# A new hand-laid order of the steps in a pooled-attention-and-two-MLPs kernel, with fourteen small steps on another engine

## The chip, the cores and the metric

One core of a Trainium2 chip. The metric is the device time of one execution of the program in microseconds (us), a median over runs. PE is the matrix engine (TensorE), DVE the vector engine, ACT the scalar engine, POOL the GpSimd engine, SP the engine that issues the DMA transfers here.

## What is computed

Pooled attention, then a gated MLP behind an RMS norm, then a second MLP, all in fp32 accuracy:

```python
k_p = k.reshape(B, H, 72, 8, D).mean(axis=3)      # B=4, H=8, S=576, D=64
v_p = v.reshape(B, H, 72, 8, D).mean(axis=3)
scores = q @ k_p.T / sqrt(D)
attn = exp(scores - scores.max(-1)); attn /= attn.sum(-1) + 1e-9
x = (attn @ v_p).transpose(0, 2, 1, 3).reshape(2304, 512)
xn = x / sqrt((x * x).mean(-1) + 1e-6) * rms_g
y = (silu(xn @ w_gate) * (xn @ w_val)) @ w_out    # 512 -> 1536 -> 512
out = silu(y @ w_in) ; out = out @ w_out2         # 512 -> 2048 -> 512
```

The reference computes silu as g / (1 + exp(-g)). The weights arrive as float64.

## The kernel before

**Tiling.** The 2304 tokens are eight chunks of 288 for the attention, with scores in pieces of 96 queries by 72 pooled keys. The gated MLP runs over chunks 0 to 4, and for the rest in two wide passes of 432 columns (called 8 and 9). The second MLP runs over three thirds of 768 tokens (a, b, c) with seven products in place of eight for a two-by-two block product. A product in fp32 accuracy is three matmuls on split numbers, high times high, high times low, low times high (`mm3`, L257 to L259; L773 in the second MLP). So each operand is split on another engine first: a rounded copy (`copy`, L237 on ACT or L239 elsewhere) and the difference from it (`combine`, L244).

**Weights.** A block of weights comes by one DMA of 512 KB of float64 words (`w_load`, L155) and is turned to fp32 by bit operations: `w_low` (L171), `w_scale` (L237), `w_sign` (on ACT L186, on DVE L178), `w_join` (L190), then the split, high (L237 or L239) and low (L244).

**Order.** Nothing orders the steps but a text. Four strings, `start`, `pair`, `last` and `second`, hold 3981 tokens; `play` goes through them and each token advances one generator by one step, which issues its instructions on their engines' queues. Each engine executes its queue in order and waits at an instruction until its inputs and its tile are there. A token is a chunk (none means 0), a letter for the kind of step, an index, and at will an engine (`:v` DVE, `:g` POOL, `:a` ACT) for its copy or difference:

```python
for o in order.split():
    o, _, e = o.partition(":")
    ...
    engine[0] = e or None
    if key not in begun:
        begun[key] = begin(*key)
    next(begun[key], None)
```

So `4H7:g` is the next step of chunk 4's eighth value tile, with its difference on POOL. The letters that matter here: K, V, Q load keys, values and queries (L276, L283 to L293, L307); k and a sum the pooled keys and values (L342 or L338, and L358 or L325 with L329) and lay them into `kbd` and `vbd`; m and s are score products (PE, L405) and the softmax's maximum (DVE, L416) and six exponentials with one small scaling (ACT, L423, L428); w divides by the sum, p transposes the weights on PE (L456), x multiplies them with the values and leaves square and raw output (L498, L237 `xraw`), r and n normalise; Z stores them. B is a weight block. G, H, D are the gate, value and output products of the first MLP; after H stands the product with the gate (L642, or L814 in a wide pass) and the split of `hT` or `hw`, which D multiplies. Y stores an MLP output (L677). Over the hand-over to the second MLP, L loads and converts a block of its output weights, S and E form their sums and splits and store them (L758), X reads the first MLP's output back (L852) and sums it (L865). A, B, C load, sum and split a block of input weights, U is its product, J and T split the hidden tile, W is the last product.

**Queues.** SP issues nearly all DMAs, in the order of the text; a load whose tile is still read, or a store whose data isn't there, holds back all behind it. Score and transposition tiles of the chunks after the first share two PSUM banks (tag `att`, two buffers): a transposition can have to wait until the exponentials have read an older score tile.

Of the kernel before, what the change touches and what calls it, by code (L numbers as in the profile page):

```python
# [22 lines left out]
def tile_pooled_attention_then_two_mlps(  # L23
# [239 lines left out]
    p1 = ctx.enter_context(tc.tile_pool(name="p1", bufs=1))  # L263
# [441 lines left out]
    p2, pw, p2x = [], [], []  # L705
# [139 lines left out]
    x2 = {}  # L845
# [148 lines left out]
    def down2(c, m):  # L994
# [112 lines left out]
    )  # L1107
# [248 lines left out]
```

## Time and profile before

| | us |
|---|---|
| median of three runs | 937.98 (937.88 to 938.92) |
| the profiled execution | 935.67 |
| its span | 933.9 |
| PE busy | 902.3 (97%), 6122 matmuls |
| DVE busy | 628.0 (67%) |
| ACT busy | 544.0 (58%) |
| POOL busy | 367.2 (39%) |

A busy share is a mean over stages that have different limits. PE's idle time (31.6 us of the span) is at the beginning, at a few waits in the middle and at the hand-over to the second MLP. A view by stretches of time gives each engine's busy time per stretch, the share of full speed that the clock of TensorE was granted (1.00 is 2.4 GHz, 0.50 is 1.2 GHz) and the share of DMA time. The view of waits says for which instruction of which engine PE waited. A timeline gives single instructions: start, length, engine, line, operation, result and operand, and in brackets the idle time before it and what ended it.

### The profile page before, as it was taken

How to read it: one execution, taken by the hardware profiler on the slowest of the kernel's cores; microseconds unless marked ns; L12 is line 12 of the kernel's file. 1: busy time of each engine (PE TensorE's matmuls, PEld its weight loads, DVE VectorE, ACT ScalarE, POOL GpSimd, SP SyncE). 2: the span in 40 equal slices, each digit the busy share in tenths (PEclk: the TensorE clock that was granted, in tenths of full speed). 3: DMA queues.
4: the chain of work that ended last, by engine and by line, in shares of the span. 5: the costliest groups of instructions: out<-in, count | busy, mean ns of one | idle time of the engine just before them, and what ended most of it. 6: DMA issues, size and time to landing. Idle time of an engine off the chain costs nothing.

```text
span 933.9 us, 17344 instructions
## 1 busy us (share of the span) xinstructions
PE 902.3 (97%) x6122; PEld 876.5 (94%) x6122; DVE 628.0 (67%) x1255; ACT 544.0 (58%) x1456; POOL 367.2 (39%) x485
## 2 busy tenths in 40 slices
PE   5999899999998999999999999999999999999998
PEld 4688899999998989999999898999999999999998
DVE  6889988756544643543466779667986669866675
ACT  5687887365252723335534546776766767667653
POOL 6544242444213541200026555892028930289200
PEclk9789999999999999999999999999999999999999
DMA  8745641442114402144466885355872568724386
GB/s 255 224 154 155 215 132 52 128 136 91 50 50 112 121 29 81 45 139 146 155 216 221 292 279 196 95 203 181 258 239 69 204 182 258 238 68 159 116 263 209
DMA packets 85259, 149.79 MB, mean 160 GB/s; under 512 B 8627, under 2 KB 53812, under 8 KB 85172
## 3 DMA queue, kind: packets, MB, share of 16 engines
q1 hardware_dynamic: 85172, 148.68, 49.5%
q8 instruction: 48, 0.79, 0.4%
q14 instruction: 39, 0.32, 0.1%
HBM read 116.21 MB, written 32.44 MB: 159 GB/s over the span
## 4 chain that ended last, share of the span: by engine, by line
PE 76%; DVE 10%; DMA 5%; POOL 3%; issue 2%; ACT 2%; SPq 1%; ACTq 0%; DVEq 0%; POOLq 0%
PE P L773 37%; PE pv L257 4%; PE pv L258 4%; PE pv L259 4%; PE pg L258 4%; PE pg L257 4%; PE pg L259 4%; PE acc L258 4%; PE acc L257 4%; PE acc L259 4%; PE sc L405 2%; DMA raw<-in_moe_w_out_dram 1%; DVE raw L178 1%; PE pT L456 1%; ACT pr L423 1%
## 5 line engine op out<-in xcount | busy, mean ns | idle before, releaser
L773 PE MATMUL P<-xP,in 128*128 128x384 f32 x1008 | 179.7, 338 | 1.4 <-POOL in L244 0.7
L773 PEld LDWEIGHTS P<-xP,in 128*128 128x128 f32 x1008 | 177.5, 188 | 2.5 <-POOL in L244 1.4
L773 PE MATMUL P<-out,hc 128*128 128x256 f32 x1512 | 172.7, 276 | 0.0
L773 PEld LDWEIGHTS P<-out,hc 128*128 128x128 f32 x1512 | 172.5, 188 | 0.0
L244 POOL TENSOR_TENSOR in<-in,in 128x256 fp32r<-128x256 f32 x96 | 77.7, 818 | 113.9 <-DVE sums L897 93.2
L237 ACT ACTIVATE hc<-h 128x384 fp32r<-128x384 f32 x144 | 74.0, 524 | 41.6 <-PE P L773 37.6
L244 DVE TENSOR_TENSOR hc<-h,hc 128x384 fp32r<-128x384 f32 x144 | 82.1, 594 | 19.7 <-ACT hc L237 16.9
L258 PE MATMUL acc<-hT,w_out 128*128 128x288 f32 x240 | 72.0, 300 | 3.0 <-POOL hT L244 2.7
L257 PE MATMUL pv<-xT,w_val 128*128 128x288 f32 x240 | 73.4, 306 | 1.2 <-DVE hT L244 1.0
L257 PE MATMUL pg<-xT,w_gate 128*128 128x288 f32 x240 | 73.1, 305 | 0.0
L257 PE MATMUL acc<-hT,w_out 128*128 128x288 f32 x240 | 73.0, 304 | 0.0
L258 PE MATMUL pg<-xT,w_gate 128*128 128x288 f32 x240 | 71.6, 299 | 0.9 <-DVE xT L244 0.9
L259 PE MATMUL acc<-hT,w_out 128*128 128x288 f32 x240 | 71.4, 297 | 0.0
L259 PE MATMUL pg<-xT,w_gate 128*128 128x288 f32 x240 | 71.3, 297 | 0.0
L258 PE MATMUL pv<-xT,w_val 128*128 128x288 f32 x240 | 70.8, 295 | 0.0
L259 PE MATMUL pv<-xT,w_val 128*128 128x288 f32 x240 | 70.8, 295 | 0.0
L624 ACT ACTIVATE th<-pg 128x288 f32<-128x288 f32 x57 | 23.4, 410 | 75.4 <-PE pg L259 75.2
L423 ACT ACTIVATE pr<-sc,mx 96x72 f32<-96x72 f32 x192 | 57.9, 316 | 14.8 <-DVE mx L416 13.2
L244 POOL TENSOR_TENSOR in<-sums,in 128x256 fp32r<-128x256 f32 x72 | 58.3, 820 | 2.9 <-ACT in L237 2.5
L626 DVE SCALAR_TENSOR_TENSOR th<-th,pg 128x288 f32<-128x288 f32 x57 | 25.5, 448 | 42.1 <-ACT th L624 42.0
L258 PEld LDWEIGHTS acc<-hT,w_out 128*128 128x128 f32 x240 | 45.7, 190 | 3.8 <-POOL hT L244 3.0
L257 PEld LDWEIGHTS pv<-xT,w_val 128*128 128x128 f32 x240 | 45.1, 188 | 2.3 <-DVE hT L244 1.5
(232 smaller groups left out, 2294.5 us busy)
## 6 DMA issues: line engine op xcount, KB each, us to landing
out<-out SPq DMA_DIRECT2D x84, 512.0 KB, 4.8
out<-out2s SPq DMA_DIRECT2D x56, 256.0 KB, 4.3
in<-in SPq DMA_DIRECT2D x24, 512.0 KB, 3.7
raw<-in_moe_w_out_dram SPq DMA_DIRECT2D x18, 512.0 KB, 4.2
raw<-in_moe_w_in_dram SPq DMA_DIRECT2D x16, 512.0 KB, 3.8
early_raw<-in_moe_w_gate_dram SPq DMA_DIRECT2D x10, 512.0 KB, 4.6
early_raw<-in_moe_w_out_dram SPq DMA_DIRECT2D x10, 512.0 KB, 5.6
early_raw<-in_moe_w_val_dram SPq DMA_DIRECT2D x10, 512.0 KB, 4.6
```

Source lines behind the costliest of these rows:

```text
L178: nc.vector.tensor_scalar(out=byte[:, :, 3], in0=byte[:, :, 7], scalar1=0x80, scalar2=None, op0=ALU.bitwise_and)
L237: nc.scalar.activation(out=out, in_=in_, func=AF.Copy, scale=1.0 if scale is None else scale)
L244: ENGINES[engine[0] or usual].tensor_tensor(out=out, in0=in0, in1=in1, op=op)
L257: nc.tensor.matmul(ps, lhsT=whi, rhs=xhi, start=first, stop=False)
L258: nc.tensor.matmul(ps, lhsT=whi, rhs=xlo, start=False, stop=False)
L259: nc.tensor.matmul(ps, lhsT=wlo, rhs=xhi, start=False, stop=last)
L405: nc.tensor.matmul(ps[:TT, a * 2 * SP:(a + 1) * 2 * SP], lhsT=qT[:, a * TT:(a + 1) * TT], rhs=kbd[:, j, :], start=True, stop=True,)
L423: nc.scalar.activation(out=pr[:, a, e], in_=s4[:, a, e], func=AF.Exp, bias=mx[:, a, e:e + 1], accum_out=sm[:, a, e],)
L456: nc.tensor.transpose(ps[:n, a * TT:(a + 1) * TT], src, ident[:TT, :TT])
L624: nc.scalar.activation(out=th, in_=pg, func=AF.Tanh, scale=0.5)
L626: nc.vector.scalar_tensor_tensor(out=th, in0=th, scalar=1.0, in1=pg, op0=ALU.add, op1=ALU.mult)
L773: nc.tensor.matmul(ps, lhsT=a, rhs=b, start=first and n == 0, stop=n == 2, skip_group_check=True)
```

## The change

Only the four strings change: the same 3981 tokens in another order. No function changes. Fourteen tokens name another engine: six differences or copies go from DVE to POOL (the low parts of three weight blocks, one `xT` difference of chunk 0, squares of chunks 1 and 5), one from ACT to POOL (the high part of a weight block); one from POOL to ACT (a value copy), one from POOL to DVE (a value sum), and four from ACT to DVE (a high part, an output copy, a raw attention output, an `hT` copy); one names DVE where DVE is the default. The longest moves: one query load of chunk 7 is issued 95 tokens later and another 49 later, a key copy of chunk 2 comes 79 later, and a gate product of wide pass 8 (`8G9`) comes 63 earlier, ahead of several output products.

Lines of the diff, at the beginning, at chunk 4's eighth value tile and at wide pass 9's third:

```diff
-        "K1 K0 Q1 B0 V5 Q0 k1 V4 k1:g k0 K2 g0 1Q0 m1 k0:g V0 1Q1 s1 a5 K3 m0 a4:v Q2 B2 B0 B0 s1 d4:g Q3 B0:v "
...
+        "B0 K1 Q1 K0 k1 Q0 V4 V5 k1:g k0 K2 m1 k0:g 1Q0 1Q1 K3 a5 s1 a4:v V0 m0 Q2 B0 B0 s1 V3 d4:g Q3 B0:v g0 "
...
-        "5w3:v 5w2:g 4G7 4H7 5x0 I5 5p5 4H7 4H7:a 4D6 5p1 5x1 5x1 4G8 5p2 5p2:a 5p5:v I5 4G8 4H8 6V5 5p5 5p3 6K1 "
-        "6a5 5p2 4G8 4H8 4H8:a 4H7:g 5p3:v 4D7 6Q1 5x2 5R0 5R1 5R2 5R3 4G9 6K0 5p3 5x3 6k1:g 6a5:v 4H9 6K3 4H8:g "
...
+        "4H6:v I4 5w3:v 5w2:g 4G7 5x0 5p5 4H7 4H7:a 4D6 5p1 5x1 5x1 4G8 5p2 5p2:a 5p5:v I5 4G8 6V5 5p5 4H7:g 5p3 "
+        "6K1 6a5 5p2 4G8 4H8 4H8 4H8:a 5p3:v 4D7 5x2 5R1 5R2 5R3 4G9 6K0 5p3 5x3 6k1:g 6k1:a 6a5:v 4H9 6K3 5R0 "
...
-        "E17 E16 L6 L7:v E17 E15 E18 E18 E19 E19 E16 9D1 E20 E17 9D1 9H2 9H2 L7 E20 9D1 S3 9H2 E18 E21 9D1 E19 "
...
+        "E17 E16 9H2 L6 E17 E15 E18 E18 E19 E19 E16 9D1 E20 E17 9D1 9H2 9H2 L7:v L7 E20 9D1 S3 E18 E21 9D1 E19 "
```

**The beginning, SP.** The first DMAs of the program, as a difference (minus before, plus after; `early_...` are the first buffers, `early_raw` those for weights).

```order
+L155 DMA early_raw_142<-in_moe_w_gate_dram 128x4x256
 L276 DMA early_125<-in_k_dram 128x576
-L276 DMA early_126<-in_k_dram 128x576
-L307 DMA early_127<-in_q_dram 128x288
-L155 DMA early_raw_142<-in_moe_w_gate_dram 128x4x256
+L307 DMA early_126<-in_q_dram 128x288
+L276 DMA early_127<-in_k_dram 128x576
+L307 DMA early_126<-in_q_dram 128x288
 L288 DMA early_128<-in_v_dram 32x512
-L307 DMA early_127<-in_q_dram 128x288
 L288 DMA early_129<-in_v_dram 32x512
```

The load of the first weight block (512 KB) moves from fourth place to first, ahead of the keys and queries. The order behind it is K1, Q1, K0, Q0, V4, V5, where it was V5, Q0, V4 before; the loads of the next weight blocks come later.

**Around 40 us, ACT.** Before, from the tile conversions of block 6 on (`sq` and `xraw` are chunk 0's or 1's attention output, `pr,sm` six exponentials, `early_raw` and `w_...` weight conversions, `xT` and `pT` copies for PE):

```order
L237 ACTIVATE early_raw_148<-early_raw_148 128x512
L498 ACTIVATE sq<-pv 128x288
L237 ACTIVATE xraw<-pv,g_sb 128x288
L237 ACTIVATE early_raw_147<-early_raw_147 128x512
L237 ACTIVATE pT<-pT 128x288
L237 ACTIVATE xT_569<-xraw 128x288
L498 ACTIVATE sq<-pv 128x288
L237 ACTIVATE xraw<-pv,g_sb 128x288
L423 ACTIVATE pr,sm<-sc,mx 96x72 x6
L428 ACTIVATE sm<-sm 96x6
L237 ACTIVATE w_gate_596<-early_raw_145 128x512
L237 ACTIVATE w_val_631<-early_raw_146 128x512
```

and after:

```order
L237 ACTIVATE early_raw_148<-early_raw_148 128x512
L237 ACTIVATE xraw<-pv,g_sb 128x288
L237 ACTIVATE xT_549<-xraw 128x288
L237 ACTIVATE xT_556<-xraw 128x288
L237 ACTIVATE pT<-pT 128x288
L423 ACTIVATE pr,sm<-sc,mx 96x72 x6
L428 ACTIVATE sm<-sm 96x6
L237 ACTIVATE early_raw_147<-early_raw_147 128x512
L498 ACTIVATE sq<-pv 128x288
L237 ACTIVATE pR<-pT 32x288
L237 ACTIVATE xraw<-pv,g_sb 128x288
L237 ACTIVATE w_gate_608<-early_raw_145 128x512
```

The exponentials of chunk 2's first scores (`pr,sm<-sc,mx`, then L428) come ahead of a weight conversion and of one pair of square and raw copy; before they stood behind both.

**Chunk 4's `hT` near 290 us, POOL.** Before (`kv` and `vs` are a value sum of chunk 6, L338 and L340 a key sum, `hT` the low part of a hidden tile that PE multiplies):

```order
L239 COPY rest<-pr 96x3x3x16 x2
L325 TENSOR_TENSOR kv<-kv 96x256
L325 TENSOR_TENSOR kv<-kv 96x128
L329 TENSOR_TENSOR vs<-kv 96x64
L244 TENSOR_TENSOR hT<-th,hT 128x288
L338 TENSOR_TENSOR kv<-kv 128x72x4
L338 TENSOR_TENSOR kv<-kv 128x72x2
L340 TENSOR_TENSOR kp<-kv 128x72
L244 TENSOR_TENSOR hT<-th,hT 128x288
```

and after:

```order
L239 COPY rest<-pr 96x3x3x16 x2
L244 TENSOR_TENSOR hT<-th,hT 128x288
L325 TENSOR_TENSOR kv<-kv 96x256
L325 TENSOR_TENSOR kv<-kv 96x128
L329 TENSOR_TENSOR vs<-kv 96x64
L338 TENSOR_TENSOR kv<-kv 128x72x4
L338 TENSOR_TENSOR kv<-kv 128x72x2
L340 TENSOR_TENSOR kp<-kv 128x72
L244 TENSOR_TENSOR hT<-th,hT 128x288
```

The `hT` difference that stood between the value sum and the key sum now stands ahead of the value sum.

**The hand-over to the second MLP, DVE.** Before, over one block of output weights (`out_...`, `out2s`) and one tile of wide pass 9 (`thw`, `hw`):

```order
L178 TENSOR_SCALAR raw<-raw 128x512
L171 TENSOR_SCALAR raw<-raw 128x512
L190 SCALAR_TENSOR_TENSOR out_6013<-raw 128x512
L178 TENSOR_SCALAR raw<-raw 128x512
L244 TENSOR_TENSOR out2s<-out_5867,out2s 128x256
L244 TENSOR_TENSOR out2s<-sums,out2s 128x256
L814 TENSOR_TENSOR thw<-thw,pv 128x432
L190 SCALAR_TENSOR_TENSOR out_6013<-raw 128x512
L244 TENSOR_TENSOR hw<-thw,hw 128x432
L244 TENSOR_TENSOR out2s<-out_6013,out2s 128x256
```

and after:

```order
L178 TENSOR_SCALAR raw<-raw 128x512
L171 TENSOR_SCALAR raw<-raw 128x512
L814 TENSOR_TENSOR thw<-thw,pv 128x432
L190 SCALAR_TENSOR_TENSOR out_6012<-raw 128x512
L244 TENSOR_TENSOR out2s<-out_5886,out2s 128x256
L244 TENSOR_TENSOR out2s<-sums,out2s 128x256
L244 TENSOR_TENSOR hw<-thw,hw 128x432
L178 TENSOR_SCALAR raw<-raw 128x512
L190 SCALAR_TENSOR_TENSOR out_6012<-raw 128x512
L244 TENSOR_TENSOR out2s<-out_6012,out2s 128x256 x2
```

The gate product `thw` (L814) goes ahead of the conversion of the block (L190, the second L178), and `hw`'s difference ahead of its last conversion. On POOL, in the same place, the split `out2s<-out` of a first sum (`E21`) now precedes the in-place difference `out<-out` (`S3`), which it followed.

## Rows read from the trace of the kernel before

**Rows 1.** The page, busy time of each engine over the whole span.
```profile
PE 902.3 (97%) x6122; PEld 876.5 (94%) x6122; DVE 628.0 (67%) x1255; ACT 544.0 (58%) x1456; POOL 367.2 (39%) x485
```

**Rows 2.** By stretches: length, busy us per engine, clock, DMA share, GB/s.
```profile
0.00:15.00 15.00, 6.29 (x22) 5.12 (x23) 9.38 (x17) 7.00 (x35) 7.60 (x21) 1.00 0.90 272
...
35.00:60.00 25.00, 24.02 (x110) 18.24 (x109) 19.53 (x44) 17.23 (x46) 7.45 (x8) 0.66 0.50 151
60.00:100.00 40.00, 34.62 (x254) 32.71 (x253) 39.31 (x78) 29.97 (x103) 18.90 (x29) 1.00 0.59 181
...
290.00:330.00 40.00, 34.67 (x249) 33.34 (x249) 20.82 (x50) 22.03 (x101) 25.23 (x43) 0.96 0.37 111
...
500.00:582.00 82.00, 78.48 (x395) 73.32 (x395) 62.94 (x104) 43.61 (x105) 49.50 (x60) 1.00 0.76 260
```

**Rows 3.** The same view by the granted clock.
```profile
36.00:53.00 17.00, 16.02 (x61) 12.14 (x61) 12.31 (x28) 9.30 (x29) 7.11 (x8) 0.50 0.46 127
53.00:100.00 47.00, 41.62 (x298) 38.40 (x298) 45.52 (x92) 36.91 (x118) 18.90 (x29) 1.00 0.59 184
...
291.95:295.36 3.41, 2.95 (x12) 2.95 (x13) 2.32 (x3) 0.00 (x0) 2.85 (x5) 0.50 0.38 97
...
333.00:934.00 601.00, 593.44 (x3944) 583.44 (x3942) 393.01 (x731) 341.81 (x777) 227.31 (x275) 1.00 0.54 176
```

**Rows 4.** PE's waits: total us, times, longest.
```profile
PE sc L405 <- POOL kbd L241: 6.9, 3, 5.4
...
PE pT L456 <- ACT xraw L237: 2.0, 2, 1.8
...
PE acc L257 <- ACT hw L237: 1.1, 1, 1.1
```

**Rows 5.** Timeline of ACT, 36 to 50 us.
```profile
44.82 0.41 ACT L498 ACTIVATE sq<-pv 128x288 f32<-128x288 f32 x1 [2.49 <-PE pv L491]
...
45.51 0.31 ACT L423 ACTIVATE pr<-sc,mx 96x72 f32<-96x72 f32 x1
```

**Rows 6.** Timeline of PE, 40 to 50 us.
```profile
47.46 0.66 PE L456 MATMUL pT<-ident,rest 96*32 96x96 f32 x3 [0.98 <-ACT pr L423]
```

**Rows 7.** Timeline of POOL, 280 to 297 us.
```profile
289.96 1.25 POOL L325 TENSOR_TENSOR kv<-kv 96x256 f32<-96x256 f32 x2 [9.23 <-DMA kv<-in_v_dram]
...
291.57 0.79 POOL L244 TENSOR_TENSOR hT<-th,hT 128x288 fp32r<-128x288 f32 x1
```

**Rows 8.** Timeline of ACT, 282 to 297 us.
```profile
283.91 0.44 ACT L237 ACTIVATE hT<-th 128x288 fp32r<-128x288 f32 x1 [1.28 <-DVE th L642]
```

**Rows 9.** Timeline of PE, 286 to 297 us.
```profile
292.41 0.61 PE L258 MATMUL acc<-hT,w_out 128*128 128x288 f32 x1 [2.74 <-POOL hT L244]
```

**Rows 10.** Timeline of DVE, 505 to 518 us.
```profile
509.93 0.76 DVE L178 TENSOR_SCALAR raw<-raw 128x512 uint8<-128x512 uint8 x1
...
510.85 1.23 DVE L190 SCALAR_TENSOR_TENSOR out<-raw 128x512 uint32<-128x512 uint32 x1
512.00 1.29 DVE L178 TENSOR_SCALAR raw<-raw 128x512 uint8<-128x512 uint8 x1
...
514.28 0.59 DVE L814 TENSOR_TENSOR thw<-thw,pv 128x432 f32<-128x432 f32 x1
```

**Rows 11.** Timeline of POOL, 505 to 525 us.
```profile
512.65 1.09 POOL L244 TENSOR_TENSOR out2s<-out,out2s 128x256 fp32r<-128x256 f32 x1
...
515.91 0.96 POOL L244 TENSOR_TENSOR out<-out 128x256 f32<-128x256 f32 x1 [0.69 <-DMA out<-out2s]
516.84 0.74 POOL L244 TENSOR_TENSOR out2s<-out,out2s 128x256 fp32r<-128x256 f32 x1
```

**Rows 12.** Chain that ended last, 495 to 582 us: start, us, what.
```profile
517.97 4.99 DMA raw<-in_moe_w_out_dram
```

**Rows 13.** Instruction groups of POOL, 0 to 130 us: count, busy, mean, idle.
```profile
L244 POOL TENSOR_TENSOR w_val<-early_raw,w_val 128x512 fp32r<-128x512 f32 x5 | 6.9, 1382 | 10.5 <-DVE w_val L239 4.4 <-issue 3.2 <-ACT w_val L237 2.9
```

**Rows 14.** Instruction groups of DVE, 0 to 130 us.
```profile
L244 DVE TENSOR_TENSOR w_val<-early_raw,w_val 128x512 fp32r<-128x512 f32 x2 | 1.3, 666 | 0.0
```

207 rows, old and new, of tables (last, pair, second, start) are left out of this document.

## The prediction

> **What bounds the kernel now.** I first read the page's busy line: PE is busy 902.3 us of a span of 933.9 [rows 1], so 31.6 us is all that an order alone can win by filling PE, and what it wins beyond comes from the clock. Next the stretches of time, to see where these 31.6 us lie. From 333 us to the end PE is busy 593.4 of 601.0 us at full clock [rows 3]; only the hand-over to the second MLP (500 to 582 us) loses 3.5 us of that [rows 2]. The start is different: in the first 15 us PE works 6.3 us, from 35 to 60 us it is busy but at a mean clock of 0.66, and from 60 to 100 us it is idle for 5.4 us while DVE is busy 39.31 of 40 [rows 2]. So the start is a chain of latencies, the stretch to 100 us is bound by DVE, and nearly all the rest by PE. Then PE's waits, which name the single places: 5.4 us for the first keys, 1.8 us for a raw output, 1.1 us for one `hw` [rows 4], and the longest behind the start, 2.74 us for one `hT` [rows 9]. Last the granted clock: half (1.2 GHz) from 36 to 53 us, and once more from 291.95 to 295.36 us [rows 3], right at the end of that wait.
>
> A measurement of this kernel can tell 0.2% from no change, that is 1.9 us.
>
> **The change part by part.** The work is the same, so only waits, the clock and the engines' shares can change. I go by the places where PE waits or where a move feeds DVE's chain.
>
> **1, the start: about -2.4 us.** The block of 512 KB goes to the head of SP's queue. At the 272 GB/s of the first 15 us [rows 2] it takes 1.93 us, so keys and queries can land up to 1.9 us later, and the wait of 5.4 us for the first keys [rows 4] can become 7.3. Against that stands ACT's new order. Before, six exponentials of chunk 2 begin at 45.51, behind a square that ACT idled 2.49 us for, until 44.82 [rows 5]; PE then waits 0.98 us for them at 47.46, with a transposition that has the first gate products of the MLP behind it [rows 6]. Afterwards the exponentials stand ahead of that square and ahead of a weight conversion, so they can use the 2.49 us. That is 2.49 us plus the conversion's, the square's and the copy's places; I estimate 3 to 4 us for the first gate product, and take off half a microsecond to a microsecond for the late keys, since ACT's own early gaps absorb most of the 1.9. What is left, 2.4 us, has to get through the DVE-bound stretch. It does so far as DVE's own work begins earlier: between 35 and 60 us DVE is idle 25.00 - 19.53 = 5.5 us [rows 2], and that is what there is to win; from 60 us on only 0.7 us is free. Bounds: +1.9 (the late keys alone, no gain) and -5.5. I take -2.4, nearer to the middle, because the one directly named wait is only 0.98.
>
> **2, the middle, 283 to 333 us: about -5.2 us.** PE's wait of 2.74 us [rows 9] ends with POOL's `hT` difference, 291.57 to 292.36 [rows 7]. Its operand, ACT's rounded `hT`, was there at 284.35 [rows 8], 7 us before. POOL did not take it up, since a value sum stood ahead in its queue, and POOL had idled 9.23 us for that sum's DMA [rows 7]. In the new order the difference stands ahead of the sum and runs in that idle time. So the wait of 2.74 us goes. The half clock from 291.95 to 295.36 begins during this gap; without a gap I expect none. In it PE's 12 instructions took 2.95 us [rows 3], half of which, 1.48, is the clock. Together 4.2 us. What is late next is the following `hT`, behind value sum and key sum as before; PE gets to it earlier by the time won, and the margin is a few tenths of a microsecond. Later in the stretch PE waits 1.8 us for a raw output [rows 4] that ACT writes after a store has released a buffer. The stores and two query loads of SP change places there, and the transposition now needs the other of two raw outputs first, but the softmax steps behind it are no earlier: I take 1.0 of the 1.8. Bounds: -2.7 (the wait goes, and the clock falls at another place) and -6.8 (all that PE is idle from 290 to 330 us, 40.00 - 34.67 = 5.3 [rows 2], and the 1.48).
>
> **3, the hand-over, 500 to 582 us: about -1.8 us.** PE loses 82.00 - 78.48 = 3.5 us [rows 2], 1.1 of it waiting for `hw` [rows 4]. That `hw` is made from a DVE product at 514.28, and DVE did two 512-wide steps of a weight block, 510.85 and 512.00, ahead of it [rows 10]; in the new order it precedes both, by 514.28 - 510.85 = 3.4 us. The 1.1 us go. But the second MLP's start hangs on the chain of weight blocks, not on this product. There POOL's split, 516.84 to 517.58, moves ahead of the difference that it followed for 0.96 us [rows 11]; its store is followed on SP by the next weight load, issued at 517.97, which took 4.99 us to land and is in the chain that ended last [rows 12]. That load goes about 0.9 us earlier, and a like swap comes one more time; I count 0.9 + 0.9. Bounds: 0 (the chain is as long by its other steps) and -3.5.
>
> **4, fourteen engines, and the rest: 0.** Seven small steps go to POOL, where a 128x512 difference takes 1.38 us [rows 13] against DVE's 0.67 [rows 14]. DVE, which bounds the stretch to 100 us, loses six and takes in five, so its sum changes by less than a microsecond; POOL is busy 18.9 of 40 us there [rows 2] and hides them. Between 100 and 285 us, from 333 to 500 and from 582 us on, PE is bound, and a moved step costs nothing as long as its result is there before PE asks. If that cover is gone, each such wait costs its own length, and a wait like [rows 9] also some 1.5 us of clock. The key sums, loads and gate products that move furthest have microseconds of lead there.
>
> **Sum:** -2.4 - 5.2 - 1.8 = -9.4 us, from the profiled execution's 935.67 to 926.3. The median of the runs shown is 937.98, 2.3 us above this execution, so I forecast 937.98 - 9.4 = **928.6 us**.
>
> **The rivals.**
> - *Only the middle pays.* The start's lead is eaten by the DVE-bound stretch, where DVE is free for 0.7 of 40 us, and the hand-over is set by DMA. For it: each load in that chain takes about 5 us [rows 12]. Against it: DVE's idle time before 60 us. Time: 937.98 - 5.2 = 932.8.
> - *DVE pays for POOL's work.* The trace shows the same 512-wide L178 step at 0.76 us at 509.93 and at 1.29 us at 512.00, the latter beside a POOL difference from 512.65 [rows 10, 11]. Five of the seven steps that go to POOL lie before 100 us; at 0.53 us each DVE loses 2.7 us where it is the bound, and the start's gain is gone: 928.6 + 2.7 = 931.3. The Trainium skill, page "SBUF — State Buffer", section "Who interferes with whom", has a rule for this: a DVE instruction with two SBUF inputs or in a two-port mode and a GpSimd instruction share one pair of ports, and whichever starts first keeps it to its end. By that rule the trace agrees so far (0.76 against 1.29).
> - *Nothing to tell.* The late keys cost 1.9 and are not made up, only the `hT` wait itself goes (-2.7), the hand-over gives nothing: -0.8, so 937.2.
> - *Slower.* PE comes to the first gate products earlier but DVE can't feed it; with a gap like the 2.74 us of [rows 9] between 48 and 100 us, the clock falls there as it did at 291.95, for a stretch like the first, 17.0 us with 16.0 us of PE work [rows 3], of which 8.0 us are lost. With the late keys (+1.9) and the middle's -5.2 it is +4.7: 942.7. It decides from the point where the low clock lasts over about 11 us more (5.2 us lost). For it: PE's 5.4 us idle between 60 and 100 us at full clock. Against it: that idle time lies in short waits, and the clock stayed at 1.00 through them [rows 3].
> - That the change doesn't do what it says is excluded by the order of the instructions: the `hT` difference does stand ahead of the sum.
>
> **How the numbers follow.** The forecast has 0.58, only the middle 0.16, the ports 0.06, nothing to tell 0.10, slower 0.10. Faster by over 0.2% takes the first three, 0.80. The bounds of the terms sum to +1.9 - 2.7 + 0 = -0.8 and -5.5 - 6.8 - 3.5 = -15.8, so 937.2 and 922.2: the range is 922 to 937, which leaves out the slower rival and little more. The likeliest case's own range is 924 to 932.
>
> **What would show it.** Right: no POOL `hT` among PE's waits of over 1 us, the granted clock 1.00 all through 285 to 300 us, the gate product after POOL's sum no later; the exponentials of chunk 2 begin near 42 us and the first gate product near 45; `hw` gone from PE's waits, PE busy over 80 of 82 us in the hand-over. Wrong: the first keys' wait grows and the stretch to 100 us ends no earlier; a new low clock between 53 and 100 us, or any new wait of over a microsecond behind 333 us.

## The result and the profile after

The changed kernel takes 922.09 us (median of 4, 920.90 to 922.41) against 937.93 (median of 4) for the one before: ratio 0.9832, 95% interval 0.9813 to 0.9851. That is 15.8 us less, where 9.4 was forecast; it lies at the very edge of the range of 922 to 937, whose bounds summed to 922.2. Against the medians of the kernel before in three later batches, 935.28 to 937.11 us, it would be 13 to 15 us less. The profiled executions differ by less too: spans of 920.3 and 933.9 us, 13.6 us, since the profiled execution of before was 2.3 us under its own median. All that follows is taken from these two traces and those of the experiments, without E9, whose profiled execution ran with PE slowed (busy 2237.5 us of a span of 2249.4).

The page, busy time of each engine, answering to [rows 1]:

```profile
PE 901.8 (98%) x6122; PEld 875.4 (95%) x6122; DVE 631.2 (69%) x1254; ACT 542.5 (59%) x1453; POOL 375.8 (41%) x487
```

PE's work is the same; its idle time fell from 31.6 to 18.5 us. By stretches, answering to [rows 2], and two stretches by the clock, answering to [rows 3]:

```profile
0.00:15.00 15.00, 6.62 (x28) 6.22 (x29) 8.93 (x16) 5.96 (x27) 7.63 (x20) 1.00 0.92 301
...
35.00:60.00 25.00, 25.00 (x114) 18.08 (x114) 18.66 (x42) 17.42 (x49) 7.46 (x10) 0.68 0.48 155
60.00:100.00 40.00, 38.96 (x286) 36.71 (x285) 39.55 (x87) 34.33 (x110) 22.02 (x31) 1.00 0.65 201
...
290.00:330.00 40.00, 39.65 (x307) 38.61 (x306) 24.41 (x62) 23.72 (x106) 25.21 (x41) 1.00 0.29 87
...
500.00:582.00 82.00, 80.29 (x414) 75.89 (x413) 68.50 (x111) 45.78 (x110) 52.54 (x59) 1.00 0.71 237
```

```profile
16.80:50.90 34.10, 32.23 (x112) 22.21 (x113) 24.14 (x54) 24.72 (x110) 18.96 (x26) 0.50 0.56 179
...
100.00:333.00 233.00, 232.37 (x1783) 230.63 (x1782) 155.72 (x359) 129.96 (x414) 94.53 (x132) 1.00 0.33 101
```

From 60 to 100 us PE is busy 38.96 us where it was busy 34.62, and DVE as busy as ever (39.55 against 39.31). The clock is at half from 16.8 to 50.9 us and at full from there to the end: the second stretch at half is gone. The 1.00 of the very first stretches can't be read as full speed, before or after: the records of the granted clock begin only at 29.1 us before and at 13.4 us after, and ahead of that PE's matmuls take as long as at half. Six score matmuls of one shape, in the kernel before, ahead of the first record and in the stretch at full behind it:

```profile
25.86 1.75 PE L405 MATMUL sc<-kbd,qT 128*96 128x144 f32 x6
...
30.28 0.95 PE L405 MATMUL sc<-kbd,qT 128*96 128x144 f32 x6
```

PE's first matmul begins at 5.4 us before and at 7.3 after. So PE ran at half for some 24 + 17 = 41 us before and 6 + 34 = 40 us after: in the start the half speed is cut up in another way, and lasts about as long as before. The prediction, which counted it from 36 us on [rows 3], left the first 24 us out. PE's waits, answering to [rows 4]:

```profile
PE sc L405 <- POOL kbd L241: 8.9, 3, 7.3
PE pT L456 <- POOL pr L244: 1.7, 1, 1.7
...
PE acc L258 <- DVE hw L244: 0.8, 1, 0.8
...
PE acc L257 <- ACT hw L237: 0.2, 1, 0.2
```

The first keys come later (7.3 against 5.4 us), the waits for POOL's `hT` and the raw output are gone, and ACT's `hw` is waited for 0.2 us where it was 1.1; a wait of 0.8 us for DVE's `hw` stays. The wait of 1.7 us for POOL's `pr`, at 17.6 us, is new.

To see where the time went, I take the same PE instructions in each trace and write down how much earlier or later (minus is earlier) each began than in the trace of before, stretch by stretch. The marks, at their time before, are the first matmul of chunk 0's first gate product (47.8 us), of chunk 1's sixth value product (109.2), of chunk 4's seventh output product (283.4) and tenth gate product (295.8), of chunk 5's fourth gate product (338.6), of pass 9's second output product (507.2) and fifth gate product (518.6), of the fifth product of the second MLP (584.5), and the end of PE's work (930.1).

| trace | to 47.8 | to 109 | to 283 | to 296 | to 339 | to 507 | to 519 | to 585 | to the end | sum |
|---|---|---|---|---|---|---|---|---|---|---|
| after | +0.7 | -4.9 | 0.0 | -4.4 | -3.0 | +0.1 | -2.0 | -0.1 | 0.0 | -13.5 |
| E1, only `start` | -1.7 | -4.7 | +1.5 | -0.7 | -0.7 | -0.1 | +1.0 | +0.3 | 0.0 | -5.2 |
| E2, before, `hT` first | +2.8 | +0.2 | +1.9 | -4.3 | +1.3 | -0.2 | +2.2 | -1.4 | 0.0 | +2.4 |
| E3, before, `thw` first | -1.2 | -0.1 | +0.4 | -0.1 | -0.6 | +1.1 | -1.6 | +1.7 | 0.0 | -0.4 |
| E4, after, block fourth | 0.0 | -4.2 | +0.5 | -4.4 | -3.1 | -0.3 | -2.0 | +0.8 | 0.0 | -12.7 |
| E5, before, three on DVE | -2.0 | +1.9 | +0.9 | -0.3 | -1.0 | -0.1 | 0.0 | -0.3 | 0.0 | -0.9 |
| E6, after, `thw` back | -0.2 | -4.6 | +1.5 | -4.4 | -3.2 | -0.2 | -0.1 | -1.8 | 0.0 | -12.9 |
| E7, after, `hT` back | +0.2 | -5.0 | +0.6 | -4.4 | -3.1 | -0.4 | -2.0 | +0.4 | -0.1 | -13.8 |
| E8, after, 30 small matmuls | +1.9 | -3.8 | 0.0 | -4.3 | -3.2 | -0.3 | -2.0 | 0.0 | -0.1 | -11.8 |
| E10, before, V5 and three | -1.2 | -3.2 | +1.8 | +1.3 | +0.3 | +0.8 | +0.2 | -0.1 | 0.0 | -0.1 |
| E11, after, engines back | -0.3 | -3.4 | +0.6 | -4.4 | -3.1 | +0.4 | -2.0 | +1.6 | 0.0 | -10.5 |
| E12, after, 12 small matmuls | -0.9 | -4.7 | +0.2 | -4.4 | -3.1 | +0.4 | -1.9 | +1.2 | -0.1 | -13.3 |

The change gains in three places, as forecast: 4.2 us up to 109 us, but all of it behind the first gate product; 7.4 us between 283 and 339; 2.0 us at the hand-over.

### The profile page after: what moved, and what is told of

Read it like the earlier page. It is cut to its first block, busy times and chain, and to the rows that moved or that the text cites. A ratio compares the mean times of both kernels' runs of the same rounds, so it can differ in the third digit from the quotient of the medians.

```text
span 920.3 us, 17356 instructions
## 1 busy us (share of the span) xinstructions
PE 901.8 (98%) x6122; PEld 875.4 (95%) x6122; DVE 631.2 (69%) x1254; ACT 542.5 (59%) x1453; POOL 375.8 (41%) x487
## 4 chain that ended last, share of the span: by engine, by line
PE 81%; DVE 9%; DMA 4%; POOL 3%; issue 2%; ACT 1%; SPq 0%; ACTq 0%; POOLq 0%; DVEq 0%
PE P L773 38%; PE pv L257 4%; PE pv L259 4%; PE pv L258 4%; PE pg L258 4%; PE pg L257 4%; PE pg L259 4%; PE acc L258 4%; PE acc L257 4%; PE acc L259 4%; PE sc L405 2%; PE pT L456 1%; PE pv L491 1%; DMA out<-out2s 1%; DMA xw_raw<-xw 1%
## 5 line engine op out<-in xcount | busy, mean ns | idle before, releaser
L624 ACT ACTIVATE th<-pg 128x288 f32<-128x288 f32 x57 | 23.5, 413 | 72.1 <-PE pg L259 71.9
L257 PEld LDWEIGHTS pg<-xT,w_gate 128*128 128x128 f32 x240 | 45.7, 190 | 1.3 <-issue 1.0
L258 PEld LDWEIGHTS pg<-xT,w_gate 128*128 128x128 f32 x240 | 45.6, 190 | 0.6 <-DVE xT L244 0.6
```

Source lines behind the costliest of these rows:

```text
L257: nc.tensor.matmul(ps, lhsT=whi, rhs=xhi, start=first, stop=False)
L258: nc.tensor.matmul(ps, lhsT=whi, rhs=xlo, start=False, stop=False)
L624: nc.scalar.activation(out=th, in_=pg, func=AF.Tanh, scale=0.5)
```

## The experiments

Single executions differ in the start: before the first gate product the traces stand between -2.0 and +2.8. Much of that goes with the clock. The traces with 10 to 17 us at full clock ahead of that product (E1, E3, E5, E10, E12) begin it at 45.8 to 46.9 us, those with 3.4 to 6.8 us at 47.5 to 50.6 (without E8, where added matmuls made PE late). So the stretches are compared, and the medians with their intervals stand beside. In the batches with E1 to E4, E5 to E8 and E9 to E12 the kernel before had medians of 935.55, 937.11 and 935.28 us.

**E1, the change's `start` alone.** The other three strings are those of before.

```diff
-    start = (the order of before)
+    start = (the order of the change)
```

> The kernel before with only the string `start` of the change (all of chunk 0 and 1's order and the weight blocks to about 110 us). In the two traces PE stands 4.2 us earlier at 110 us, and it stood even at 55 us, so the theory is that `start` alone gives 4.2 us, all of it between 65 and 105 us: 929.6 to 930.4 for the span against 933.9, and the wait of 2.74 us for `hT` near 290 us still there. Rival (the prediction's own reason): the gain is the earlier first gate product, 2.4 us, and PE is already ahead at 55 us.

Measured: 929.87 us, ratio 0.9947 (0.9927 to 0.9966). Up to 109 us it gains 6.4, of which 4.7 behind the first gate product, and 5.2 are left at the end. So the one string carries 4 to 5 us, and it does so from 48 to 109 us, in a stretch in which DVE is full in both kernels.

**E2, `hT` first, in the kernel before.**

```diff
-5p5:v I5 4G8 4H8 6V5 5p5 5p3 6K1 6a5 5p2 4G8 4H8 4H8:a 4H7:g 5p3:v
+5p5:v I5 4G8 4H8 6V5 5p5 4H7:g 5p3 6K1 6a5 5p2 4G8 4H8 4H8:a 5p3:v
```

> The kernel before with one step moved: the low part of chunk 4's eighth hT goes ahead of the value sum on POOL. Theory: the wait of 2.74 us goes and with it the half clock of 3.41 us behind it, 4.2 to 4.4 us in all: span 929.5 to 929.7. Rival: the clock falls anyway in this stretch, so only 2.7 us goes (931.2); or POOL's later steps come late instead and the time stays within 1 us of 933.9.

Measured: 934.12 us, ratio 0.9976 (0.9949 to 1.0003), and in its trace 4.3 us gained between 283 and 296, as expected for this stretch. In POOL's timeline the difference now runs ahead of the sum, and the clock over this stretch is full:

```profile
289.39 0.81 POOL L244 TENSOR_TENSOR hT<-th,hT 128x288 fp32r<-128x288 f32 x1 [3.76 <-ACT hT L237]
294.72 1.28 POOL L325 TENSOR_TENSOR kv<-kv 96x256 f32<-96x256 f32 x2 [4.52 <-DMA kv<-in_v_dram]
```

```profile
285.00:295.00 10.00, 10.00 (x80) 9.99 (x79) 5.43 (x14) 3.51 (x9) 1.40 (x3) 1.00 0.52 150
```

The expected span of 929.5 to 929.7 us did not come. The trace is 2.8 us late already in the start, and 2.2 us are lost at 519, where `hw` is waited for 1.9 us and the clock falls for 3.4 us. Between 296 and 339 it loses 1.3 us, in a new wait of 1.4 us for POOL's `sq` at 303 us: PE is early there, and the result is not. The interval of the medians, -4.8 to +0.3 us, holds both the 4.3 us and nothing; that the stretch's gain reaches the end isn't shown.

**E7, `hT` back, in the changed kernel.** The same pair of steps the other way round.

```diff
-4G8 6V5 5p5 4H7:g 5p3 6K1 6a5 5p2 4G8 4H8 4H8 4H8:a 5p3:v
+4G8 6V5 5p5 5p3 6K1 6a5 5p2 4G8 4H8 4H8 4H8:a 4H7:g 5p3:v
```

> The changed kernel with chunk 4's eighth hT difference back between value sum and key sum on POOL. Theory: PE's wait returns, though shorter than 2.74 us where the DMA for the value sum lands earlier, and with it a half clock of 3.4 us if the wait is over about 2 us: 924.5 to 926.5 in all. Rival: in the new order the DMA lands early enough, POOL is not held, and the time stays at 922.1.

Measured: 921.42 us, ratio to before 0.9830 (0.9794 to 0.9866); the 4.4 us stay. The rival held. POOL still takes up the difference behind the sum, but the sum is no longer late:

```profile
282.54 1.27 POOL L325 TENSOR_TENSOR kv<-kv 96x256 f32<-96x256 f32 x2 [7.01 <-DMA kv<-in_v_dram]
283.88 0.32 POOL L329 TENSOR_TENSOR vs<-kv 96x64 f32<-96x64 f32 x1
284.16 0.81 POOL L244 TENSOR_TENSOR hT<-th,hT 128x288 fp32r<-128x288 f32 x1
```

With this trace 4.1 us ahead of that of before, the sum that began at 289.96 [rows 7] would begin at 285.8; it began at 282.54. Its load is issued earlier in the change, since a store ahead of it on SP (its DVE step was moved ahead) is ready earlier. The load before, and in E7:

```profile
283.29 0.75 SPq L293 DMA_DIRECT2D kv<-in_v_dram  x1
```

```profile
275.76 0.75 SPq L293 DMA_DIRECT2D kv<-in_v_dram  x1
```

So the swap that I had named ends the wait by itself (E2) and isn't needed in the change, where the rest of the order keeps the wait away. That it does so by the earlier load is read from the traces; the load was not moved alone.

**E3 and E6, `thw` first in the kernel before, and back in the changed one.**

```diff
-E17 E16 L6 L7:v E17 E15 E18 E18 E19 E19 E16 9D1 E20 E17 9D1 9H2 9H2 L7 E20 9D1 S3 9H2 E18
+E17 E16 9H2 L6 L7:v E17 E15 E18 E18 E19 E19 E16 9D1 E20 E17 9D1 9H2 9H2 L7 E20 9D1 S3 E18
```

That is E3: one token, the third `9H2`, moves to the front. E6 moves it back in the changed kernel.

> The kernel before with one step of the hand-over moved: the gate product of wide pass 9's third tile and its split go ahead of the weight block's conversion on DVE; the swap of split and difference on POOL is not made. Theory from the two traces, where PE gains 1.96 us just at this tile: about 1.5 to 2 us. Rival (the prediction's reason): the chain of weight blocks sets the hand-over, so the time won at this tile is lost again by 580 us and the time stays within 0.5 us.

> The changed kernel with wide pass 9's third gate product and its split back behind the weight block on DVE; the rest of the hand-over stays as changed. Theory (the chain of weight blocks and sums sets the hand-over): PE loses 1.5 to 2 us at this tile and has most of it back at the first product of the second MLP, the end is within 0.6 us of 922.1. Rival (PE's wait at the tile is what counts): the loss stays, 923.5 to 924.1.

Measured: E3 936.55 us, ratio 1.0017 (0.9988 to 1.0045); E6 921.75, ratio 0.9840 (0.9810 to 0.9870). The two agree: with the product ahead, PE has 1.6 us more at 519 and loses 1.7 of it by 585; with the product back in the changed kernel, PE has 1.9 less at 519 and wins 1.8 by 585. At the first product of the second MLP it makes no difference. So this product is not what sets that point. The traces with the rest of the change's hand-over gain 0.4 to 2.1 us from 507 to 585, those without it between a gain of 0.3 and a loss of 1.3: the change wins there by other steps, and they weren't tried one by one.

**E4, the first weight block's load in fourth place.**

```diff
-"B0 K1 Q1 K0 k1 Q0 V4 V5
+"K1 Q1 K0 B0 k1 Q0 V4 V5
```

> The changed kernel with the first weight block's load back in fourth place on SP, behind the first keys and queries. Theory: the wait for the first keys falls from 7.3 to 5.4 us, and the half clock that began at 16.8 us begins later or lasts shorter, so PE is 1 to 2 us ahead by 50 us; what remains at the end is between 0 and -2 us against 922.1. Rival: the stretch from 60 to 105 us absorbs it, and the time is within 0.5 us of 922.1, or the late weight block delays the first gate products and it is up to 2 us slower.

Measured: 921.55 us, ratio 0.9845 (0.9813 to 0.9876) against 0.9832 for the change. The first gate product comes 0.7 us earlier than in the change, at 109 us nothing is left of it. In these traces the late keys cost nothing in the end.

**E8 and E12, PE at work while it waits.** Ahead of the score products of chunks 0 and 1 there are matmuls of the identity matrix with itself, whose result the real product overwrites.

```diff
+    def warm(c, ps, n):
+        if c < 2:
+            for _ in range(n):
+                nc.tensor.matmul(ps[:, :P], lhsT=ident, rhs=ident, start=True, stop=True)
...
+        warm(c, ps, {(0, 1): 30, (0, 0): 4}.get((c, j), 5))
```

In E12 the last line is `{(0, 1): 12}.get((c, j), 2)`.

> The changed kernel with small 128x128 matmuls ahead of each score product of the first two chunks (30 ahead of the first, 4 or 5 ahead of the others), into the score tile that the real product then overwrites: PE works while it would wait for the first keys and queries. In the changed kernel TensorE had half its clock from 16.8 to 50.9 us, and PE was busy 25.00 of 25 us from 35 to 60 us. Theory (the clock bounds this stretch): with PE at work from the beginning the clock is full earlier, PE is 3 to 8 us ahead at the first gate product, and 2 us or more of it are left at 110 us: 914 to 920. Rival: the chain of exponentials on ACT and DVE's work set the start; the end is within 1 us of 922.1, or up to 2 us later since the small matmuls delay the real ones.

> The changed kernel with fewer of the small matmuls: 12 ahead of the first score product, 2 ahead of each other one of the first two chunks. The run with 30 had the full clock from 6.1 to 36.8 us but its small matmuls ended at 10.9 us, 3.6 us behind the first keys' arrival at 7.3, and PE was only 1.2 us late at the first gate product: so 2.4 us had been won back by the clock. Theory: with 12 of them, ended by about 7 us, the clock is still full from about 6 us and PE is 1 to 2.4 us earlier at the first gate product, the end 920 to 921.5. Rival (ACT and DVE set the start): the time stays within 0.7 us of 922.1.

Measured: E8 924.11 us, ratio 0.9864 (0.9834 to 0.9894); E12 922.61, ratio 0.9875 (0.9843 to 0.9907). The clock does as wished in part. In E12, by its stretches:

```profile
8.19:18.43 10.24, 6.87 (x54) 6.06 (x52) 8.66 (x17) 7.69 (x50) 8.35 (x15) 1.00 1.08 366
18.43:28.67 10.24, 9.54 (x34) 6.99 (x34) 6.58 (x16) 7.45 (x38) 9.94 (x14) 0.50 0.24 80
28.67:35.50 6.83, 5.61 (x35) 3.67 (x34) 6.20 (x15) 6.77 (x34) 5.51 (x7) 1.00 0.94 280
35.50:49.15 13.65, 13.65 (x50) 9.84 (x50) 9.77 (x21) 8.37 (x28) 4.37 (x5) 0.50 0.59 211
```

Behind its first stretch at full, half speed lasts 23.9 us there, in two pieces, instead of 34.1. The first gate product comes 1.6 us earlier than in the change, which is within the spread of single executions, and PE is 1.4 us ahead at 109 us. But the lead doesn't reach the end: 0.4 us of it go by 507, and the rest between 519 and 585, at the hand-over, where a lead was lost in E3 too. In E8 PE was late by its small matmuls, and stayed so. Neither kernel is faster than the change; the rivals held.

**E5, three weight differences from POOL to DVE, in the kernel before.** These are the seventh steps of blocks 7, 10 and 13.

```diff
-B7 ... B10 ... B13
+B7:v ... B10:v ... B13:v
```

> The kernel before with the low parts of three weight blocks between 65 and 97 us (128x512, 1.4 us each on POOL) done on DVE, where each takes about 0.67 us. Three DVE instructions that ran beside these POOL differences took 1.56, 1.58 and 1.81 us, where the same instructions took 0.44, 0.43 and 0.81 in the changed kernel, beside none. Theory (DVE waits for POOL, and the change gains by setting them apart): the three are back at 0.44, 0.43 and about 0.7, DVE gets 2.0 us more work and 3.4 us less waiting, and PE is 1 to 1.5 us earlier from 75 to 110 us. Rival (order alone): the three stay long, DVE gets 2.0 us more, and PE is up to 2 us later at 110 us. The start differs by some us between executions, so the difference from 55 to 110 us counts.

Measured: 935.07 us, ratio 0.9989 (0.9966 to 1.0011). Here are the three DVE instructions in the kernel before, and what POOL did beside each:

```profile
65.83 1.56 DVE L244 TENSOR_TENSOR th<-th,early_x 128x288 f32<-128x288 f32 x1
...
90.44 1.58 DVE L239 CAST w_out<-early_raw 128x512 fp32r<-128x512 f32 x1
...
95.78 1.81 DVE L190 SCALAR_TENSOR_TENSOR early_raw<-early_raw 128x512 uint32<-128x512 uint32 x1
```

```profile
65.68 1.39 POOL L244 TENSOR_TENSOR w_val<-early_raw,w_val 128x512 fp32r<-128x512 f32 x1 [0.34 <-ACT w_val L237]
...
90.42 1.31 POOL L244 TENSOR_TENSOR w_val<-early_raw,w_val 128x512 fp32r<-128x512 f32 x1 [3.20 <-issue]
...
95.62 1.42 POOL L244 TENSOR_TENSOR w_val<-early_raw,w_val 128x512 fp32r<-128x512 f32 x1
```

and the same three in E5, where the POOL differences are gone:

```profile
63.09 0.45 DVE L244 TENSOR_TENSOR th<-th,early_x 128x288 f32<-128x288 f32 x1
```

```profile
91.96 0.43 DVE L239 CAST w_out<-early_raw 128x512 fp32r<-128x512 f32 x1
```

```profile
96.50 0.68 DVE L190 SCALAR_TENSOR_TENSOR early_raw<-early_raw 128x512 uint32<-128x512 uint32 x1
```

The theory held for the instructions, 4.95 us became 1.56. For PE it held from 76 to 109 us, where the last two of them lie: it gained 1.5 us. Two waits for DVE's `pT`, in the kernel before

```profile
94.74 0.47 PE L456 MATMUL pT<-ident,pr 96*128 96x96 f32 x3 [1.05 <-DVE pT L244]
...
98.38 0.40 PE L258 MATMUL pv<-pT,vbd 128*128 128x288 f32 x1 [1.42 <-DVE pT L244]
```

are one in E5:

```profile
95.60 0.47 PE L456 MATMUL pT<-ident,pr 96*128 96x96 f32 x3 [0.50 <-DVE pT L244]
```

But 3.4 us were lost between the first gate product and 76 us, in a wait of 2.9 us for POOL's `ms` and a stretch at half clock around it (65.0 to 71.9 us), so PE is 1.9 us worse at 109, and the median shows no gain. The edit did not make this loss: the second half of a value sum on POOL, a step of 96x128 with a mean of 0.66 us in the trace of before, took 3.96 us while DVE ran ten instructions without a gap, and `ms` stood behind it. The first of the moved differences came on DVE only when that was over but for 0.03 us:

```profile
59.89 3.96 POOL L325 TENSOR_TENSOR kv<-kv 96x128 f32<-96x128 f32 x1
63.93 0.75 POOL L329 TENSOR_TENSOR vs<-kv 96x64 f32<-96x64 f32 x1
64.64 0.86 POOL L537 TENSOR_TENSOR ms<-ms,mhalf 96x3 f32<-96x3 f32 x1
```

```profile
63.82 0.68 DVE L244 TENSOR_TENSOR w_val<-early_raw,w_val 128x512 fp32r<-128x512 f32 x1
```

E2, with the order of before up to there, has a wait of 2.3 us at the same place. That POOL was held by DVE is read from the times alone.

**E9 and E10, V5's load ahead of a store.** E9 moves one token, E10 has E5's edit too.

```diff
-1p5 B6 1x2 n0 B9 ... G0 B5 2V5 1x1:v
+1p5 B6 1x2 2V5 n0 B9 ... G0 B5 1x1:v
```

> The kernel before with one load moved: the sixth value load of chunk 2 (V5) goes ahead of the store on SP that waits for ACT until 52.8 us; it was issued at 54.0 us, behind that store, and POOL idled 11.2 us for it, with chunk 1's ms step queued behind its sum. Theory (the gain of `start` is made of single results that stood behind such a step): the wait of PE for POOL's ms (0.9 us here, 2.3 and 2.9 us in two other executions with this start) goes, the stretch from the first gate product to 110 us is 0.9 to 2 us shorter. Rival: DVE is full there and takes the time back; the stretch stays within 0.4 us.

> The kernel before with V5 ahead of the store and the three weight differences on DVE. Theory: both parts add, DVE's long instructions beside POOL are gone (3.4 us less, 2.0 us more work), and the stretch from the first gate product to 110 us is 2 to 4 us shorter, near the 4.2 to 4.9 us that the whole of `start` gives. Rival (the order of DVE's own steps is what counts): it is shorter by 1 us at most.

Measured: E9 933.33 us, ratio 0.9982 (0.9958 to 1.0006); no trace shows its stretch, so the expectation stays open. E10 934.81, ratio 0.9991 (0.9965 to 1.0016), and in its trace 3.2 us gained from the first gate product to 109. The wait behind it, in the kernel before, by SP, POOL and PE:

```profile
52.76 0.25 SPq L556 DMA_DIRECT2D rs<-early_x  x1
...
53.96 0.80 SPq L293 DMA_DIRECT2D kv<-in_v_dram  x1
```

```profile
61.04 2.06 POOL L325 TENSOR_TENSOR kv<-kv 96x256 f32<-96x256 f32 x2 [11.17 <-DMA kv<-in_v_dram]
...
63.79 1.55 POOL L537 TENSOR_TENSOR ms<-ms,mhalf 96x3 f32<-96x3 f32 x1
```

```profile
65.40 0.91 PE L542 MATMUL rs<-ident,ms 96*128 96x96 f32 x6 [0.92 <-POOL ms L537]
```

The load stood behind the store of `rs` (L556), which ACT's result released at 52.7; POOL's value sum waited for the load, and the `ms` step stood behind the sum, with PE's matmuls waiting for that. In the change the load goes at 40.80:

```profile
40.80 0.90 SPq L293 DMA_DIRECT2D kv<-in_v_dram  x1
```

and in E10 POOL has done sum and `ms` by 59.3, ahead of what PE needs:

```profile
51.59 1.60 POOL L325 TENSOR_TENSOR kv<-kv 96x256 f32<-96x256 f32 x2 [2.79 <-issue]
...
58.16 1.11 POOL L537 TENSOR_TENSOR ms<-ms,mhalf 96x3 f32<-96x3 f32 x1 [4.48 <-DVE ms L533]
```

So two small edits of the kernel before give 3.2 of the 4.2 to 5.0 us that the change's start gives there in five traces (the change, E1, E4, E6 and E7). Of these, 1.7 us are won by 76 us, about the `ms` step; which of the two edits gives them isn't separated, since the first of the three differences lies there too. The other 1.5 come from 76 to 109, as in E5. E10 is no faster all the same, since PE, now 2.6 us ahead at 283, meets the `hT` wait there, which is set by a DMA: it grew to 3.7 us, and the half clock to 6.8 us:

```profile
290.10:296.90 6.80, 6.10 (x25) 6.10 (x26) 3.69 (x5) 0.80 (x2) 3.09 (x5) 0.50 0.46 120
```

**E11, the change's order on the engines of before.** All fourteen tokens have their old engine.

> The changed kernel's order with the fourteen steps on the engines of before. Theory (the order carries the gain): the end is within 1.5 us of 922.1, the middle and the hand-over give what they gave, and only the stretch to 110 us can lose 0 to 1.5 us. Rival (the engines carry it, since they free DVE): more than 2 us of the 4.2 to 4.9 us to 110 us are lost, 924 or more.

Measured: 922.59 us, ratio 0.9868 (0.9836 to 0.9900). The order carries the gain: of the 4.2 to 5.0 us up to 109, 3.4 are left, and the middle is untouched. In this trace 1.6 us more are lost at the hand-over, with a stretch at half clock; the medians don't show it.

## Why the prediction was right, and where it was wrong

**1, the start: the sign was right, the step failed.** The prediction put 2.4 us on an earlier first gate product ("the exponentials of chunk 2 begin near 42 us and the first gate product near 45"). They begin at 45.34 and 48.52:

```profile
45.34 0.31 ACT L423 ACTIVATE pr<-sc,mx 96x72 f32<-96x72 f32 x1
```

```profile
48.52 0.59 PE L257 MATMUL pg<-xT,w_gate 128*128 128x288 f32 x1
```

That is as late as before [rows 5, 6]. The step that failed is to take ACT's exponentials for the bound. From 16.8 to 50.9 us PE is busy 32.2 of 34.1 us at half clock, so PE itself was the bound there, and ACT's better order couldn't be used; in the kernel before PE was busy 16.02 of 17.00 us at half too [rows 3]. The traces with more time at full clock have the first gate product earlier, as told above. The gain of 4.2 us came where the prediction had ruled one out, from 60 to 109 us, "bound by DVE" and with 0.7 us free. DVE is full there, but its sum isn't fixed: the 111 DVE instructions between 55 and 112 us that stay on DVE took 61.8 us before and 58.2 after, and 3.3 of these 3.6 us are the three instructions of E5 (0.45, 0.43 and 0.81 us in the change). And PE's single waits for DVE (1.05 and 1.42 us for `pT`, 0.81 for `hT`, 0.66 and 0.29 for `xT`) went; one of 0.82 for `hT` came new at 63.1 us. E5 and E10 show it for `pT`. For `hT` and `xT` it is only argued: in the change DVE does what PE waits for ahead of weight conversions that nobody needs yet. The wait for POOL's `ms` (0.92) went as well, and it is gone in E10.

The rival on the ports had the right mechanism with the wrong sign: it was before that DVE paid for POOL's work. E5 shows that the long instructions are long because of POOL's, and that this costs PE time; that POOL can be the one that is held is only likely. The Trainium skill, page "SBUF — State Buffer", section "Who interferes with whom", gives the rule for it (DVE with two SBUF inputs, or in a two-port mode, and GpSimd share a pair of ports, held to the end of an instruction), and these traces agree: 1.56 us for a difference beside POOL and 0.45 us alone. POOL's 3.96 us in E5 go beyond it: DVE ended ten instructions meanwhile, and a hold to the end of one does not explain that. The change has such a place too, a shift with one input (the second of the two here) beside POOL's difference of block 12:

```profile
94.19 1.88 DVE L171 TENSOR_SCALAR early_raw<-early_raw 128x512 uint32<-128x512 uint32 x2
```

```profile
94.41 1.38 POOL L244 TENSOR_TENSOR w_gate<-early_raw,w_gate 128x512 fp32r<-128x512 f32 x1 [0.42 <-POOL vbd L244]
```

**2, the middle: right in mechanism, too small in size.** The `hT` wait and its half clock were put at 4.2 us and gave 4.4, and no other stretch at half came. What failed is the raw output's place: 1.0 of 1.8 us was taken, and 3.0 us were gained from 296 to 339, so the middle's 7.4 us lie beyond its own bound of 6.8. The wait of 1.8 is gone and so are small ones of 0.2 to 0.3 us ahead of it; which of the moved stores and loads does it wasn't tried. In the five other traces with the old order there this wait was 0.5 to 1.5 us, so part of the 1.8 is the single execution's. The reason given for the `hT` wait was only one of two: E2 shows that the swap is enough for it, E7 that it isn't needed.

**3, the hand-over: right in size.** 1.8 us were forecast, 2.0 gained, though other traces with the same steps there gained less, down to 0.4 (E11). That `hw` doesn't set the point is shown by E3 and E6; that the chain of weight blocks does was not tried. That the chain is shorter by the swap of split and difference on POOL, as the prediction had it, is only argued: POOL does the split ahead of the difference now, but the swap alone wasn't tried.

**4, the engines: nearly free, as said.** E11 gives 0.8 to 1.6 us up to 109 us for them, in one trace, and no median tells it.

**The first rival** (only the middle pays, 932.8) and **the slower one** fell: E1 shows 4 to 5 us from the start, and no half clock came behind 50.9 us. The late keys cost nothing that could be seen (E4).

**The number.** By the traces the three places gave 4.2, 7.4 and 2.0 us where 2.4, 5.2 and 1.8 were forecast, and the median fell by 2.3 us more, since the profiled execution of before lay that far under its own. The likeliest range, 924 to 932, was missed. That the wider one held, by a tenth of a microsecond, is luck: the start gained by another way than the one named, and the middle more than its bound.

## What to carry to other kernels

An engine that is busy 98% of a stretch can still give time there: look at what stands in its queue ahead of the result that PE waits for, and at which of its instructions are longer than their like, and what runs beside them. When one wait has two possible causes, take the edit out of the changed kernel as well as putting it into the old one: here the wait went with the edit, and stayed away without it. And a lead lasts only to the next point that another chain or a DMA sets, so fix those points first or the gain ahead of them is not seen, as in E10 and E12.

## What had not been expected of the hardware

How long two engines can hold each other: in E2 a DVE difference of 128x288 that takes 0.45 us took 2.66 us beside two POOL steps in a row, and in E5 a POOL step of 0.66 us took 3.96. And the kernel before gave 929.5 to 940.7 us in 25 executions of one batch, the four variants of the changed kernel without added work (E4, E6, E7, E11) 918.3 to 925.2 in 16; the traces differ mostly in the first 50 us, and there by the clock: without E8, they begin the sixth group of score products at 18.0 to 18.9 us, and the first gate product at 45.8 to 50.6.
